# Converting weights in 512-word pieces on three engines, a two-step PReLU, a gram in two row tiles, and a first product from 256 tokens

## The chip, the cores and the metric

One core of a Trainium2 chip runs the whole program. The metric is the device time of one execution in microseconds (us). A profile is one execution taken with the trace; its *span* is the time that the records cover, some 1.7 us less than the time of the same run. Engines: PE is TensorE (matmul), PEld its weight load, DVE is VectorE, ACT is ScalarE, POOL is GpSimd, SP (SPq) issues transfers. A run counts as slow when it is over 1.5% above the fastest of the same kernel; ratios use the fast runs alone.

## The reference

Two stages. First a state-space scan (4 batches, 8 heads, 768 tokens, head size 32, state size 16): in each chunk a "gram" C·Bᵀ is multiplied by a matrix of decay products and applied to x, and a state is carried from chunk to chunk. Its 3072 x 256 result feeds a feed-forward block:

```python
def _moe_ref(x, w_in, w_out, alpha):          # 3072x256, 256x2048, 2048x256, 2048
    h = x @ w_in
    g = np.maximum(h, 0.0) + alpha * np.minimum(h, 0.0)
    return (g @ w_out).astype(np.float32)
```

`w_in` and `w_out` arrive in 64-bit floats, so that the kernel must make 32-bit floats of raw words on the chip. alpha lies between 0 and 0.3.

## The kernel before

A *pair* is two chunks of 128 tokens of the scan. A *group* is two pairs, 512 tokens: 16 hidden tiles (the first product, two matmuls each into one PSUM tile), then 64 matmuls of the second product (27.6 us). An fp32 matmul shows as two records in the trace, so a hidden tile is four, and a group's second product 128. There are six groups. While PE works on one group's hidden tiles, the pairs of the next are mixed in; the stretch of a group with one such pair and eight hidden tiles is called a *half*.

```python
ps_s = ...(name="ps_s", bufs=4, space=PSUM)   # everything of the scan
ps_h = ...(name="ps_h", bufs=2, space=PSUM)   # hidden tiles
ps_o = ...(name="ps_o", bufs=2, space=PSUM)   # output tiles
# ... weights: 32 pieces of 256 words: seven VectorE steps, then one add on GpSimd
# ... gram: four row tiles of 32 rows, for both chunks at once
m = work.tile([P, 2, H, Q], F32, name="m")
gram = [ps_s.tile([P, 2, 2 * Q], F32, name="ss") for r in range(4)]
# ... m = gram * dec on VectorE, four steps
def hidden(g, q):
    for j in range(FQ):
        # ... two matmuls into hp
        nc.scalar.activation(out=gt[:, j], in_=hp, func=ACTF.Relu)
        nc.scalar.activation(out=neg, in_=hp, func=ACTF.Relu, scale=-1.0)
        nc.vector.scalar_tensor_tensor(out=gt[:, j], in0=neg, scalar=nalpha[:, f : f + 1],
                                       in1=gt[:, j], op0=ALU.mult, op1=ALU.add)
# ... main loop
for i in range(GC // 2):          # both pairs of the first group, then all of w_in
    ssm(i); weights(in_pieces, i, GC // 2)
for g in range(NG):               # only then hidden tiles, 512 tokens each
    ...
```

Of the kernel before, what the change touches and what calls it, by code (L numbers as in the profile page):

```python
# [10 lines left out]
U32 = mybir.dt.uint32  # L11
ALU = mybir.AluOpType
ACTF = mybir.ActivationFunctionType

F64_INF, F64_ZERO = (struct.unpack("f", struct.pack("I", w))[0] for w in (0x47F00000, 0x38000000))
# [4 lines left out]
def kernel(  # L20
# [45 lines left out]
    wld = ctx.enter_context(tc.tile_pool(name="wld", bufs=3))  # L66
    wtp = ctx.enter_context(tc.tile_pool(name="wtp", bufs=2))
    lda = ctx.enter_context(tc.tile_pool(name="lda", bufs=2))
    ldx = ctx.enter_context(tc.tile_pool(name="ldx", bufs=4))
# [11 lines left out]
    def load_batch(b):  # L81
        ahn = ld.tile([P, S], F32, name="ahn")
        first = a[b, 0:1, :]
        nc.sync.dma_start(
            out=ahn, in_=bass.AP(tensor=first.tensor, offset=first.offset,
                                 ap=[[S, H], [0, N], [1, S]]))
        loads["b", b] = ahn

# [6 lines left out]
    def load_pair(gp):  # L95
        b, c = divmod(2 * gp, CPB)
        nat = ldx.tile([P, 2, 2, H * N], F32, name="nat")
        abc = lda.tile([P, 2, H * Q], F32, name="abc")
        xt = ldx.tile([P, 2, HD], F32, name="xt")
        for k in range(2):  # L100
            sl = slice((c + k) * Q, (c + k + 1) * Q)
            for i, src in enumerate((B, C)):
                nc.sync.dma_start(out=nat[:, i, k].rearrange("p (h n) -> p h n", h=H),
                                  in_=src[b, :, sl, :].rearrange("h p n -> p h n"))
            first = a[b, 0:1, sl]
            nc.sync.dma_start(
                out=abc[:, k].rearrange("p (h t) -> p h t", h=H),
                in_=bass.AP(tensor=first.tensor, offset=first.offset, ap=[[0, P], [S, H], [1, Q]]),
            )
            nc.sync.dma_start(out=xt[:, k].rearrange("p (h d) -> p h d", h=H),  # L110
                              in_=x[b, :, sl, :].rearrange("h p d -> p h d"))
        loads["p", gp] = nat, abc, xt

    load_rows(0)
    load_batch(0)
# [4 lines left out]
    al_n = const.tile([NF, P], F32, name="al_n")  # L120
    nc.sync.dma_start(out=al_n, in_=moe_alpha.rearrange("(k p) -> k p", p=P))
    in_pieces = [
        (w_in[:, k, f0 : f0 + WQ], moe_w_in[k * P : (k + 1) * P], f0)
        for f0 in range(0, d_ff, WQ)
        for k in range(KC)
    ]
    out_pieces = [(w_out[:, f], moe_w_out[f * P : (f + 1) * P], 0) for f in range(NF)]

    def load_weights(dst, src, c0):



        w = dst.shape[-1]
        if src.dtype == F32:
            nc.sync.dma_start(out=dst, in_=src[:, c0 : c0 + w])
            return
        raw = wld.tile([P, WQ, 2], U32, name="raw")
        nc.sync.dma_start(out=raw[:, :w].rearrange("p w t -> p (w t)"),
                            in_=src[:, c0 : c0 + w].bitcast(U32))
        lo, hi = raw[:, :w, 0], raw[:, :w, 1]  # L140
        t = wtp.tile([P, WQ], U32, name="wt")[:, :w]
        r = wtp.tile([P, WQ], U32, name="wr")[:, :w]
        d = dst.bitcast(U32)
        tf = t.bitcast(F32)


        nc.vector.tensor_single_scalar(out=t, in_=hi, scalar=0x7FFFFFFF, op=ALU.bitwise_and)
        nc.vector.tensor_scalar(out=tf, in0=tf, scalar1=F64_INF, scalar2=F64_ZERO,
                                op0=ALU.min, op1=ALU.max)
        nc.vector.tensor_scalar(out=r, in0=t, scalar1=3, scalar2=0x3FFFFFF8,  # L150
                                op0=ALU.logical_shift_left, op1=ALU.bitwise_and)
        nc.vector.scalar_tensor_tensor(out=r, in0=t, scalar=0x40000000, in1=r,  # L152
                                       op0=ALU.bitwise_and, op1=ALU.bitwise_or)
        nc.vector.scalar_tensor_tensor(out=r, in0=hi, scalar=0x80000000, in1=r,
                                       op0=ALU.bitwise_and, op1=ALU.bitwise_or)
        nc.vector.scalar_tensor_tensor(out=r, in0=lo, scalar=29, in1=r,  # L156
                                       op0=ALU.logical_shift_right, op1=ALU.bitwise_or)
        nc.vector.tensor_scalar(out=t, in0=lo, scalar1=28, scalar2=1,
                                op0=ALU.logical_shift_right, op1=ALU.bitwise_and)
        nc.gpsimd.tensor_tensor(out=d, in0=r, in1=t, op=ALU.add)  # L160
# [15 lines left out]
    par = const.tile([P, 2], F32, name="par")  # L176
    bm2 = bmask.rearrange("p (k e d) -> p e k d", e=2, d=D)
    for e in range(2):
        nc.vector.tensor_reduce(out=par[:, e : e + 1], in_=bm2[:, e, :, 0], op=ALU.add,
                                axis=mybir.AxisListType.X)  # L180
# [3 lines left out]
    nalpha = const.tile([P, NF], F32, name="nalpha")  # L184
    alp = ps_s.tile([P, 512], F32, name="ss")
    nc.tensor.transpose(alp[:, :NF], al_n, ident[:NF, :NF])
    nc.vector.tensor_scalar(out=nalpha, in0=alp[:, :NF], scalar1=-1.0, scalar2=None,
                            op0=ALU.mult)


    pre = {}
# [22 lines left out]
    def batch_prep(b):  # L214

        ahn = loads.pop(("b", b))
        d0 = prep.tile([P, S], F32, name="d0")
        d1 = prep.tile([P, S], F32, name="d1")
        nc.vector.tensor_scalar(out=d0, in0=ahn, scalar1=1e-6, scalar2=1.0,
                                op0=ALU.max, op1=ALU.min)  # L220
        nc.gpsimd.memset(d1, 0.0)
        nc.vector.tensor_copy(out=d1[:, ::Q], in_=d0[:, ::Q])
        nc.vector.memset(d0[:, ::Q], 0.0)
        pf = bat.tile([P, S], F32, name="pf")
        nc.vector.tensor_tensor_scan(out=pf, data0=d0, data1=d1, initial=0.0,
                                     op0=ALU.mult, op1=ALU.add)
        pre[b] = pf

    def pair(gp):

        b, c = divmod(2 * gp, CPB)
        if c == 0:
            batch_prep(b)
        pf = pre[b]
        nat, abc, xt = loads.pop(("p", gp))
# [3 lines left out]
        nc.gpsimd.tensor_scalar(out=abc, in0=abc, scalar1=1.0, scalar2=1e-6,  # L239
                                op0=ALU.min, op1=ALU.max)  # L240
        nc.gpsimd.memset(abc[:, :, ::Q], 0.0)  # L241
        dec = work.tile([P, 2, H, Q], F32, name="dec")
        for k in range(2):
            nc.vector.tensor_tensor_scan(out=dec[:, k].rearrange("p h t -> p (h t)"),  # L244
                                         data0=abc[:, k], data1=ident_h, initial=0.0,
                                         op0=ALU.mult, op1=ALU.add)
# [11 lines left out]
        cz = work.tile([P, 2, 2, Q], F32, name="cz")  # L258
        for e in range(2):
# [3 lines left out]
                                in1=pf[:, c * Q : (c + 2) * Q], op=ALU.mult)  # L263
# [18 lines left out]
        for k in range(nk):  # L282
# [4 lines left out]
            e = (c + k + 1) * Q - 1  # L287
# [6 lines left out]
        m = work.tile([P, 2, H, Q], F32, name="m")  # L294
        gram = [ps_s.tile([P, 2, 2 * Q], F32, name="ss") for r in range(4)]
        for k in range(2):
            for r in range(4):
                rs = slice(32 * r, 32 * r + 32)
                nc.tensor.matmul(gram[r][:, k], bh[rs, k], cz[rs, :, k], start=True, stop=True,  # L299
                                 tile_position=(32 * r, 0), skip_group_check=True)  # L300
        for r in range(4):
            hs = slice(2 * r, 2 * r + 2)
            nc.vector.tensor_tensor(out=m[:, :, hs].rearrange("p k h t -> p k (h t)"), in0=gram[r],  # L303
                                    in1=dec[:, :, hs].rearrange("p k h t -> p k (h t)"),
                                    op=ALU.mult)
# [9 lines left out]
        for k in range(2):  # L315
            for w in range(KC):
                for q in range(4):
                    h = 4 * w + q
                    nc.tensor.matmul(y[32 * q : 32 * q + 32, w, k], xt[:, k, h * D : (h + 1) * D],  # L319
                                     m[:, k, h], start=False, stop=True,  # L320
# [10 lines left out]
    def hidden(g, q):  # L331
        gt = gp.tile([P, FQ, GT], F32, name="gt")
        for j in range(FQ):
            f = q * FQ + j
            hp = ps_h.tile([P, GT], F32, name="hp")
            for k in range(KC):
                nc.tensor.matmul(hp, w_in[:, k, f * P : (f + 1) * P], xts[g][:, k],  # L337
                                 start=(k == 0), stop=(k == KC - 1))
            neg = op.tile([P, GT], F32, name="neg")
            nc.scalar.activation(out=gt[:, j], in_=hp, func=ACTF.Relu)  # L340
            nc.scalar.activation(out=neg, in_=hp, func=ACTF.Relu, scale=-1.0)  # L341
            nc.vector.scalar_tensor_tensor(out=gt[:, j], in0=neg, scalar=nalpha[:, f : f + 1],  # L342
                                           in1=gt[:, j], op0=ALU.mult, op1=ALU.add)
        gts[g, q] = gt
# [15 lines left out]
    def ssm(gp):  # L360
        if gp + 1 < NP:
            load_pair(gp + 1)
        if gp % 3 == 1 and gp // 3 + 1 < batch:
            load_batch(gp // 3 + 1)
# [6 lines left out]
    def weights(lst, i, n):  # L371
        for p in lst[i * len(lst) // n : (i + 1) * len(lst) // n]:
            load_weights(*p)

    for i in range(GC // 2):
        ssm(i)
# [39 lines left out]
```

## Time and profile before

| | before |
|---|---|
| time, median of 3 | 495.63 us (494.58 to 495.81) |
| span of the profiled run | 492.1 us |
| first hidden matmul starts | 54.49 us |
| first group's output ends (last second product of group 1) | 164.66 us |
| from there to the end, "the second part" | 327.44 us |

Busy times by stretch, of the kernel before. The columns are the stretch, its length, then busy us and number of instructions of PE, PEld, DVE, ACT and POOL, then PE's granted clock, the share of the transfer engines, and GB/s:

```profile
0.00:54.49 54.49, 26.48 (x140) 16.96 (x140) 41.01 (x93) 7.40 (x20) 21.53 (x29) 0.84 0.80 180
54.49:164.66 110.17, 83.42 (x313) 49.99 (x312) 103.89 (x222) 21.00 (x40) 39.27 (x38) 0.83 0.54 123
164.66:492.10 327.44, 317.70 (x1451) 209.88 (x1451) 129.78 (x172) 98.34 (x189) 13.16 (x16) 1.00 0.12 28
```

The reader should compare PE and DVE with the length. In the middle stretch DVE is busy 103.89 of 110.17 us and PE 83.42 at a clock of 0.83: DVE bounds. In the last PE is busy 317.70 of 327.44 us: PE bounds.

### The profile page before, as it was taken

What the parts mean: (1) busy time and instruction counts of PE and PEld (TensorE: products, weight loads), DVE (VectorE), ACT (ScalarE), POOL (GpSimd) and SP (SyncE); (2) the same over time, 40 slices, a digit from 0 to 9 for tenths busy, and PEclk for the clock granted to TensorE, in tenths of its full rate; (3) what the DMA queues carried; (4) which work ended last, traced back from release to release, by engine and by line L of the source; (5) the groups of instructions that cost most, each with busy time, mean ns of one, the idle gap of its engine ahead of it and who ended that gap; (6) DMA issues with size and microseconds to landing.
All of it is one profiled execution on the core that took longest, in us unless ns stands there. A gap on an engine that the chain in (4) does not pass through costs nothing.

```text
span 492.1 us, 5000 instructions
## 1 busy us (share of the span) xinstructions
PE 427.6 (87%) x1899; PEld 276.8 (56%) x1899; DVE 274.7 (56%) x485; ACT 126.7 (26%) x249; POOL 74.0 (15%) x81
## 2 busy tenths in 40 slices
PE   0574865983879998999999999999999899999997
PEld 0343433432448644688454886446884448854685
DVE  2699997999899959401877105593024530024300
ACT  2010301420230163400346102643004450046300
POOL 2553543225132210101021000000000000000000
PEclk9985967995699999999999999999999999999999
DMA  6978878544314333200534000000000000000000
GB/s 128 216 170 184 178 185 157 107 118 149 71 38 147 82 92 47 82 23 21 91 60 107 1 22 23 0 1 1 23 21 0 1 0 1 21 23 0 0 23 21
DMA packets 108536, 32.42 MB, mean 66 GB/s; under 512 B 76048, under 2 KB 103904, under 8 KB 108512
## 3 DMA queue, kind: packets, MB, share of 16 engines
q1 hardware_dynamic: 108512, 32.10, 28.4%
q8 instruction: 15, 0.25, 0.2%
q14 instruction: 9, 0.07, 0.1%
HBM read 28.94 MB, written 3.15 MB: 65 GB/s over the span
## 4 chain that ended last, share of the span: by engine, by line
PE 58%; DVE 2%; ACT 0%; issue 0%
PE po L353 28%; PE hp L337 25%; PE ss L319 2%; PE ss L312 1%; DVE m L303 1%; PE ss L276 1%; PE ss L299 1%; PE ss L253 0%; DVE dm L278 0%; DVE state L288 0%; DVE gt L342 0%; ACT gt L340 0%; ACT neg L341 0%; DVE cd L262 0%; DVE o_sb L355 0%
## 5 line engine op out<-in xcount | busy, mean ns | idle before, releaser
L337 PE MATMUL hp<-xT,w_in 128*128 128x512 f32 x384 | 174.8, 605 | 5.2 <-ACT neg L341 5.1
L353 PE MATMUL po<-w_out,gt 128*128 128x256 f32 x768 | 170.2, 381 | 6.8 <-POOL w_out L160 5.8
L353 PEld LDWEIGHTS po<-w_out,gt 128*128 128x128 f32 x768 | 145.8, 191 | 33.9 <-POOL w_out L160 11.2
L337 PEld LDWEIGHTS hp<-xT,w_in 128*128 128x128 f32 x384 | 71.7, 191 | 89.1 <-issue 64.2
L342 DVE SCALAR_TENSOR_TENSOR gt<-neg,nalpha,gt 128x512 f32<-128x512 f32 x96 | 79.4, 833 | 66.9 <-ACT neg L341 66.5
L340 ACT ACTIVATE gt<-hp 128x512 f32<-128x512 f32 x96 | 57.3, 597 | 123.2 <-PE hp L337 123.2
L355 DVE COPY o_sb<-po 128x256 f32<-128x256 f32 x24 | 10.1, 421 | 122.5 <-PE po L353 122.4
L341 ACT ACTIVATE neg<-hp 128x512 f32<-128x512 f32 x96 | 56.8, 592 | 13.5 <-DVE gt L342 13.5
L244 DVE TENSOR_TENSOR_SCAN dec<-abc,ident_h 128x1024 f32<-128x1024 f32 x24 | 55.4, 2337 | 1.6 <-POOL abc L241 1.0
L299 PE MATMUL ss<-cz,bh 32*128 32x256 f32 x192 | 32.8, 464 | 19.3 <-DVE cd L262 16.0
L257 ACT COPY bh<-ss 128x256 f32<-128x256 f32 x12 | 4.5, 375 | 141.9 <-PE ss L253 141.9
L299 PEld LDWEIGHTS ss<-cz,bh 32*128 32x128 f32 x192 | 20.1, 211 | 34.2 <-DVE cd L262 19.0
L239 POOL TENSOR_SCALAR abc<-abc 128x2048 f32<-128x2048 f32 x12 | 25.2, 2098 | 85.4 <-DMA abc<-in_a_dram 71.6
L303 DVE TENSOR_TENSOR m<-ss,dec 128x512 f32<-128x512 f32 x48 | 30.4, 681 | 2.2 <-PE ss L299 2.2
L269 POOL TENSOR_TENSOR bn<-nat,prt 128x256 f32<-128x256 f32 x12 | 10.6, 883 | 85.7 <-PE ss L276 52.5
L319 PE MATMUL ss<-m,xt 128*32 128x128 f32 x384 | 21.1, 310 | 1.9 <-DVE m L303 1.9
L160 POOL TENSOR_TENSOR w_out<-wr,wt 128x256 uint32<-128x256 uint32 x16 | 15.8, 985 | 43.4 <-DVE wr L156 43.4
L325 ACT COPY xT<-ss 128x512 f32<-128x512 f32 x12 | 7.1, 589 | 55.8 <-PE ss L319 55.8
L160 POOL TENSOR_TENSOR w_in<-wr,wt 128x256 uint32<-128x256 uint32 x16 | 16.4, 1023 | 29.6 <-DVE wr L156 29.5
L319 PEld LDWEIGHTS ss<-m,xt 128*32 128x32 f32 x384 | 12.1, 118 | 12.8 <-issue 6.1
L312 PE MATMUL ss<-cd,state 128*128 128x128 f32 x64 | 11.1, 326 | 8.4 <-DVE m L303 8.4
L152 DVE SCALAR_TENSOR_TENSOR wr<-wt,wr 128x256 uint32<-128x256 uint32 x32 | 16.7, 521 | 0.0
(47 smaller groups left out, 183.4 us busy)
## 6 DMA issues: line engine op xcount, KB each, us to landing
abc<-in_a_dram SPq DMA_DIRECT2D x24, 512.0 KB, 5.0
raw<-in_moe_w_in_dram SPq DMA_DIRECT2D x16, 256.0 KB, 3.9
raw<-in_moe_w_out_dram SPq DMA_DIRECT2D x16, 256.0 KB, 2.6
xt<-in_x_dram SPq DMA_DIRECT2D x24, 128.0 KB, 3.3
out_dram<-o_sb SPq DMA_DIRECT2D x12, 256.0 KB, 2.1
ahn<-in_a_dram SPq DMA_DIRECT2D x4, 384.0 KB
nat<-in_B_dram SPq DMA_DIRECT2D x24, 64.0 KB, 3.1
nat<-in_C_dram SPq DMA_DIRECT2D x24, 64.0 KB, 2.8
```

Of the source, the lines that this page charges most:

```text
L152: nc.vector.scalar_tensor_tensor(out=r, in0=t, scalar=0x40000000, in1=r, op0=ALU.bitwise_and, op1=ALU.bitwise_or)
L160: nc.gpsimd.tensor_tensor(out=d, in0=r, in1=t, op=ALU.add)
L239: nc.gpsimd.tensor_scalar(out=abc, in0=abc, scalar1=1.0, scalar2=1e-6, op0=ALU.min, op1=ALU.max)
L244: nc.vector.tensor_tensor_scan(out=dec[:, k].rearrange("p h t -> p (h t)"), data0=abc[:, k], data1=ident_h, initial=0.0, op0=ALU.mult, op1 ...
L299: nc.tensor.matmul(gram[r][:, k], bh[rs, k], cz[rs, :, k], start=True, stop=True, tile_position=(32 * r, 0), skip_group_check=True)
L303: nc.vector.tensor_tensor(out=m[:, :, hs].rearrange("p k h t -> p k (h t)"), in0=gram[r], in1=dec[:, :, hs].rearrange("p k h t -> p k (h t)"),
L319: nc.tensor.matmul(y[32 * q : 32 * q + 32, w, k], xt[:, k, h * D : (h + 1) * D], m[:, k, h], start=False, stop=True, tile_position=(0, 32 ...
L337: nc.tensor.matmul(hp, w_in[:, k, f * P : (f + 1) * P], xts[g][:, k], start=(k == 0), stop=(k == KC - 1))
L340: nc.scalar.activation(out=gt[:, j], in_=hp, func=ACTF.Relu)
L341: nc.scalar.activation(out=neg, in_=hp, func=ACTF.Relu, scale=-1.0)
L342: nc.vector.scalar_tensor_tensor(out=gt[:, j], in0=neg, scalar=nalpha[:, f : f + 1], in1=gt[:, j], op0=ALU.mult, op1=ALU.add)
L353: nc.tensor.matmul(po[:, :d_model], gts[g, f // FQ][:, f % FQ, ts], w_out[:, f], start=(f == 0), stop=(f == NF - 1))
```

## The change

Its intent: relieve VectorE in the first part (bigger pieces, three steps in place of seven on it), start PE earlier (256 tokens, two weight pieces), and relieve ScalarE and VectorE in the PReLU and the gram. Cut to its core:

```diff
-        nc.vector.tensor_single_scalar(out=t, in_=hi, scalar=0x7FFFFFFF, op=ALU.bitwise_and)
 ...    (six more VectorE steps for 256 words)
-        nc.gpsimd.tensor_tensor(out=d, in0=r, in1=t, op=ALU.add)
+        nc.scalar.activation(out=tf, in_=hi.bitcast(F32), func=ACTF.Abs, scale=0.125)
+        nc.vector.tensor_scalar(out=tf, in0=tf, scalar1=F64_INF, scalar2=F64_ZERO, ...)
+        nc.scalar.activation(out=g, in_=half, func=ACTF.Copy, scale=2.0**-11, bias=2.0**25)
+        if sg is None:      # w_in
+            nc.gpsimd.tensor_scalar(out=r, in0=hi.bitcast(F32), scalar1=0.0, scalar2=2.0**31,
+                                    op0=ALU.is_lt, op1=ALU.mult)          # the sign
+        else:               # w_out
+            for i in range(2):
+                nc.vector.tensor_scalar(out=r[:, i], in0=hi[:, i], scalar1=SIGN, scalar2=sg[i], ...)
+        nc.vector.scalar_tensor_tensor(out=r, in0=t, scalar=3, in1=r, ...)  # shift and combine
+        nc.vector.tensor_tensor(out=d, in0=r, in1=g.bitcast(U32), op=ALU.add)

-            nc.scalar.activation(out=gt[:, j], in_=hp, func=ACTF.Relu)
-            nc.scalar.activation(out=neg, in_=hp, func=ACTF.Relu, scale=-1.0)
-            nc.vector.scalar_tensor_tensor(out=gt[:, j], in0=neg, scalar=nalpha[:, f : f + 1],
-                                           in1=gt[:, j], op0=ALU.mult, op1=ALU.add)
+            nc.scalar.mul(gt, hp, s_alpha[:, f : f + 1])
+            nc.vector.scalar_tensor_tensor(out=gt, in0=hp, scalar=s_mul[:, f : f + 1], in1=gt,
+                                           op0=ALU.mult, op1=ALU.max)

-        gram = [ps_s.tile([P, 2, 2 * Q], F32, name="ss") for r in range(4)]
 ...    (16 matmuls of 32 rows; product into m)
+        for k in range(2):
+            gram = [ps_s.tile([P, 4, Q], F32, name="ss") for r in range(2)]
 ...        (two matmuls of 64 rows)
+                nc.vector.tensor_tensor(out=dec[:, k, hs], in0=gram[r], in1=dec[:, k, hs], ...)

+    ssm(0)
+    for q in range(NQ):     # two w_in pieces, then four hidden tiles of 256 tokens; pair 1 after q = 0
+        ...
+    for q in range(NQ):     # two w_out pieces, then the other 256 tokens; pairs 2 and 3 between
+        ...
```

The whole diff holds smaller parts too: the decays are loaded and scanned for each pair and no longer for each batch, GpSimd clamps the decays of one chunk at a time, the first loads of B and C go to ScalarE's queue, and two pools change their number of buffers.

## The prediction

> **What bounds the kernel now**
>
> I read the strip of 40 slices first, to see whether one engine bounds the whole span, and then busy times by stretch.
>
> ```profile
> PE   0574865983879998999999999999999899999997
> ...
> DVE  2699997999899959401877105593024530024300
> ...
> PEclk9985967995699999999999999999999999999999
> DMA  6978878544314333200534000000000000000000
> ...
> 50.00:75.00 25.00, 19.48 (x77) 10.54 (x75) 24.38 (x56) 5.07 (x10) 13.23 (x12) 0.78 0.83 186
> ...
> 100.00:125.00 25.00, 13.82 (x38) 7.36 (x38) 24.39 (x57) 2.15 (x4) 9.71 (x10) 0.74 0.41 122
> ...
> 271.60:299.20 27.60, 27.60 (x130) 24.25 (x130) 2.20 (x5) 1.08 (x2) 0.00 (x0) 1.00 0.03 10
> 299.20:338.30 39.10, 38.34 (x188) 19.26 (x186) 27.66 (x34) 19.36 (x38) 1.66 (x2) 1.00 0.02 8
> ```
>
> There are two kernels in one. Up to about 150 us DVE is at 9 nearly throughout (24.4 of 25 us) while PE has holes and runs at a clock of 0.59 to 0.9: DVE bounds. From then on PE is full at clock 1.00 and bounds. The chain that ended last says the same: from 188 us on it is almost only PE.
>
> ```profile
> 271.59 27.63 PE po L353 x128
> 299.21 0.44 PE ss L253 x4
> 299.65 0.43 PE ss L276 x2
> 300.08 0.86 PE hp L337 x2
> 300.94 1.31 PE ss L299 x14
> 302.25 0.69 DVE m L303
> ...
> 302.98 1.16 PE ss L312 x8
> ...
> 306.54 12.21 PE hp L337 x28
> ```
>
> A group of 512 tokens is 27.63 us of second product, then twice a half of one pair's scan work mixed with eight hidden tiles. A hidden tile is four records, 27.47/16 = 1.717 us. From 299.21 to 306.54 is 7.3 us with one hidden tile in it, then seven tiles, 12.2: a half is 19.5, a group 66.6 us.
>
> What DVE does in the first part, and what it holds in the second:
>
> ```profile
> L342 DVE SCALAR_TENSOR_TENSOR gt<-neg,nalpha,gt 128x512 f32<-128x512 f32 x96 | 79.4, 833 | 66.9 <-ACT neg L341 66.5
> ...
> L154 DVE SCALAR_TENSOR_TENSOR wr<-raw,wr 128x256 uint32<-128x256 uint32 x32 | 13.6, 426 | 0.0
> ...
> L150 DVE TENSOR_SCALAR wr<-wt 128x256 uint32<-128x256 uint32 x32 | 11.6, 361 | 0.0
> ...
> 304.81 4.47 DVE L244 TENSOR_TENSOR_SCAN dec<-abc,ident_h 128x1024 f32<-128x1024 f32 x2
> 309.20 1.39 DVE L342 SCALAR_TENSOR_TENSOR gt<-neg,nalpha,gt 128x512 f32<-128x512 f32 x2
> 311.32 0.75 DVE L342 SCALAR_TENSOR_TENSOR gt<-neg,nalpha,gt 128x512 f32<-128x512 f32 x1 [0.74 <-ACT neg L341]
> ```
>
> The reader should see that two decay scans (4.47 us) hold up two PReLU steps until 309.20, and that PE doesn't notice (12.21 us without a gap): DVE doesn't free the PSUM tile today, ScalarE does.
>
> **What the Trainium skill says**
>
> - "VectorE: DVE Perf Modes", the perf-mode tier table: in fp32 a one-input op between SBUF tiles runs at 2×, a two-input one or one with a PSUM operand at 1×. The trace agrees: starts of undisturbed 256-word one-input ops lie 0.20 us apart, of two-input ones 0.34.
> - "SBUF — State Buffer", Who interferes with whom: DVE ops in a 2-port mode or with two SBUF inputs lock out GpSimd reads and the reverse. It agrees: one POOL add in the conversion took 2.97 us at 30.70 beside a scan, against 0.73 alone; one DVE op 1.98 against 0.28 beside a POOL clamp of 2.02.
> - "ScalarE: Activation LUTs", What ACT_TABLE_LOAD costs: a per-partition pointer operand adds about 93 ns. The 128x256 cz step with a pointer is 486 ns, the bh copy without 375: agrees. So the new ScalarE step is about 0.60 + 0.09 = 0.69 us.
> - "TensorE: Matmul & The Clock Gate", Part 3, Packing small matmuls: row tiles overlap. The 16 gram records of a pair ran in 1.15 us when nothing held them; one after the other they would take 16 x 0.213 = 3.4. With two row tiles instead of four I estimate 3.4/2 = 1.7 us.
>
> **The change part by part**
>
> *Conversion.* Before: 32 pieces, each four one-input and three two-input DVE ops, start to start 4 x 0.20 + 3 x 0.34 = 1.82 us, 58 us (84 us as the groups sum, with GpSimd's lock). After: 16 pieces of 512 words; on DVE a clamp (about 0.34), a shift-and-combine (0.60, as a 128x512 two-input op: 2.48/4 at 302.23) and an integer add now on DVE, which no row shows; I take 0.60. 1.54 us; for w_out two sign steps of 0.20 more. 8 x 1.54 + 8 x 1.94 = 28 us: 30 us less DVE, in the part that DVE bounds. ScalarE gets 32 steps of 0.6, 19 us, into an engine at 2 to 5 us of 25; GpSimd gets eight sign steps in place of 32 adds.
>
> *Order.* The first product now starts with 256 tokens and two pieces instead of after two pairs and all of w_in (54.5 us in the trace). By the built order the queue brings 0.06 MB of rows and alpha, two pairs of 1.7 MB, two pieces of 0.52 MB: 4.5 MB. With DMA full (share 1.00 in 12 to 25 us) the trace moved 220 GB/s: 20.5 us, plus 2 for the start, plus about 4 for conversion: 27 us.
> From there I added up DVE's built order, line by line with the start-to-start times, to the last decay product of pair 3: 8 us for the rest of pair 1, 3 + 8 + 6 for the other w_in pieces, the first half of the PReLU steps (about 0.36 each at 256 tokens) and pair 2, 14 and 20 for w_out, the second half and pair 3: 59 us, so 86 us. DMA must bring 8.4 MB of weights and some 7.7 MB of pairs by the last piece: 16.1/0.22 = 73 us when full, 91 us at the 0.8 share it had from 25 to 75. I take the later, 91. Then PE still has some 48 second products (0.432 each, 21) and the end of pair 3 (5): the first group's output ends at about **117 us**, against 164.6 before. The gain here is **48 us**. PE's own work to there is 27.5 + 27.6 + 4 x 5.4 = 77 us; before it was busy 110 us for it, 33 of them from the low clock, and idle 55.
>
> *PReLU.* Two ScalarE steps and a DVE step become one and one. ScalarE's 114 us (96 x 2 steps) become 80 x 0.69 plus 32 half ones, about 70. But the DVE step now reads the PSUM tile itself: with two such tiles, PE may fill the third only when DVE is through with the first. Cycle: 1.717 fill + 0.69 + about 0.72 on DVE + some 0.15 of handovers = 3.28, under 2 x 1.717 = 3.43. So PE stays the bound, with only 0.15 us to spare. The decay product is now written in place, so the next scan into that buffer waits for PE's last use of it, and in DVE's order both scans stand just before the second PReLU step of the half. From the end of the pair's matmuls: scans until 4.5, PReLU until 5.3; PE fills two tiles until 3.43 and then waits: **1.9 us** per half. Six halves have such scans (pairs 6 to 11): 11.5 us.
>
> *Gram.* 1.7 for 1.15 to 1.5 us on PE, and cz four steps for two on ScalarE (off the path). DVE's order also puts two short scans and a PReLU step ahead of the first decay product; I get 7.75 us from the pair's transposes to its last matmul, against 7.4. Eight halves x 0.35 = 3 us.
>
> Sum after the first group: a group is 2 x (7.75 + 1.9 + 12.0) + 27.6 = 71 us three times, 67 for the fourth, 55.1 for the last, 3.6 of tail, and 1 for odds: 339 to **340 us**, against 327.5 before (492.1 - 164.6). 117 + 340 = 457 us of span. Timed runs lie 3.5 us over the span (495.63 to 492.1): **460 us**, 7% faster.
>
> **The rivals**
>
> 1. *DVE becomes the bound of the second part too.* For: it now frees every hidden tile, has 37 us of work in a 43 us stretch, and long scans stand in its order. Against: the cycle of 3.28 fits. If the PReLU step takes 0.9 us instead of 0.72, the cycle is 3.46 and costs little; if each scan stalls PE by its full 4.4 us, add 6 x 2.5 = 15: 475.
> 2. *The first part doesn't shrink, as DMA or handovers bound it.* For: a piece passes ScalarE, GpSimd and DVE, each in strict order with only two buffers, and DMA was at 0.83 already. If the first group ends at 140, 483: within 2% nearly.
> 3. *The first part shrinks to its DVE sum.* DMA kept full, PE warm: 105 us, 448.
> 4. *Stalls don't show*, because the scans start before PE is through: then 446.
>
> **Range and chances**
>
> Rivals 1 and 2 together would be needed for no gain. The first part carries the larger doubt (105 to 135), the second part 10 us either way: 443 to 478. Faster by over 2% means under 485.7.
>
> **What would show each step right or wrong**
>
> Right: the first hidden matmul at about 27 us; DVE conversion near 28 us; first group's output ending at 117; then PE waiting for the DVE PReLU step about 2 us once per half, right after the scans, in groups 1 to 3 and not in the last two; groups of 71 us. Wrong: a group still at 66.6 (the stall is hidden), PE waits at every hidden tile (the cycle is over 3.43), PE clock low or DMA share under 0.7 in the first 90 us (waits, not work, bound the first part), or an integer add well over 0.6.

## The result, and the profile after

The changed kernel took **472.66 us** (median of 4 runs, 471.05 to 473.84), all correct, against 495.5 us for the kernel before in the same rounds: ratio 0.954, 95% interval 0.951 to 0.957. Ratios here are the mean time of one kernel's fast runs over that of the other's of the same rounds, so they aren't quite the ratio of the medians. The predicted class was right, and 472.66 lies inside the range of 443 to 478, but 12.7 us above the 460 predicted.

The strip of 40 slices of the changed kernel, 11.8 us each (busy tenths; PEclk the granted clock):

```profile
PE   1788679999989799998989998989999999999996
DVE  2998779899584830065840065840043530034200
PEclk9868889999999999999999999999999999999999
DMA  9995668935643430034330030000000000000000
```

PE is now nearly full from the seventh slice on, where before it was from about the thirteenth. But DVE isn't at 9 in slices five and six (7 and 7), nor is DMA (6 and 6), and the clock is still low there: something waits. And later PE has slices at 8 where the kernel before had 9s. Busy times by stretch:

```profile
0.00:30.26 30.26, 15.11 (x64) 7.78 (x65) 19.96 (x34) 9.62 (x24) 16.10 (x23) 0.87 0.95 195
30.26:72.00 41.74, 31.62 (x121) 17.96 (x120) 32.44 (x57) 18.82 (x37) 19.01 (x15) 0.81 0.66 176
72.00:128.89 56.89, 55.45 (x290) 41.92 (x291) 49.92 (x86) 17.76 (x37) 14.18 (x17) 1.00 0.68 156
128.89:471.60 342.71, 324.08 (x1396) 203.79 (x1393) 130.92 (x188) 73.93 (x128) 13.60 (x24) 1.00 0.14 30
```

The first group's output ends at 128.89 us, 35.8 us earlier than before (117 was predicted: 47.7). The second part takes 342.71 us, 15.3 more than before (340 was predicted: 12.6 more). So of 35.8 us won, 15.3 are given back. Two questions follow: what costs the missing 12 us in the first part, and is it the PReLU that gives back the 15 in the second?

**First part.** Between 30.26 and 72 us DVE is busy only 32.44 of 41.74 us and PE 31.62. Timeline of all engines in that stretch (start, length, engine, line, what it does; in brackets the idle time just before, and what ended it):

```profile
46.01 4.92 POOL L167 TENSOR_SCALAR wr<-raw 128x512 uint32<-128x512 f32 x2 [6.47 <-DVE w_in L176]
49.06 1.11 DVE L173 SCALAR_TENSOR_TENSOR wr<-wt,wr 128x512 uint32<-128x512 uint32 x1 [1.85 <-POOL wr L167]
50.97 0.69 DVE L173 SCALAR_TENSOR_TENSOR wr<-wt,wr 128x512 uint32<-128x512 uint32 x1 [0.80 <-POOL wr L167]
52.11 2.72 PE L352 MATMUL hp<-xT,w_in 128*128 128x256 f32 x8 [4.13 <-DVE gt L356]
```

This is a ping-pong. GpSimd waits 6.47 us for DVE's add to give back one of two sign buffers, makes two signs in 4.92 us, DVE waits for each, and the PReLU steps (L356) stand behind them in DVE's order, so that PE waits 4.13 us. The sign step by itself, its eight records as minimum, median and maximum in ns:

```profile
L167 POOL TENSOR_SCALAR wr<-raw x8: 1937/2032/3011, 22.4 to 59.7; 128x512 uint32<-128x512 f32 x8
```

Even the quickest took 1.94 us.

**Second part.** One half of the third group (PE L352 are hidden matmuls, DVE L258 the decay scans, DVE L356 the PReLU):

```profile
209.66 3.70 PE L352 MATMUL hp<-xT,w_in 128*128 128x512 f32 x8
209.85 4.47 DVE L258 TENSOR_TENSOR_SCAN dec<-abc,ident_h 128x1024 f32<-128x1024 f32 x2 [0.27 <-PE ss L332]
...
214.43 1.40 DVE L356 SCALAR_TENSOR_TENSOR gt<-hp,s_mul,gt 128x512 f32<-128x512 f32 x2
...
215.22 7.25 PE L352 MATMUL hp<-xT,w_in 128*128 128x512 f32 x16 [1.87 <-DVE gt L356]
```

PE fills two hidden tiles while the scans run, then waits 1.87 us until DVE has got to the PReLU of the first. Five other halves show the same wait, 1.66 us each; the halves of the last two groups have no scans beside them, and no such wait. The six add to 10.2 us.

### The profile page after: what moved, and what is told of

Same layout as the page of the kernel before. It is cut to its first block, busy times and chain, and to the rows that moved or that the text cites. A ratio compares the mean times of both kernels' runs of the same rounds, so it can differ in the third digit from the quotient of the medians.

```text
span 471.6 us, 4815 instructions
## 1 busy us (share of the span) xinstructions
PE 426.3 (90%) x1867; PEld 271.4 (58%) x1867; DVE 233.2 (49%) x363; ACT 120.1 (25%) x225; POOL 62.9 (13%) x78
## 3 DMA queue, kind: packets, MB, share of 16 engines
HBM read 28.94 MB, written 3.15 MB: 68 GB/s over the span
## 4 chain that ended last, share of the span: by engine, by line
PE 66%; DVE 15%; issue 9%; ACT 3%; DMA 3%; POOL 2%; SPq 0%; DVEq 0%; POOLq 0%; ACTq 0%
PE po L366 31%; PE hp L352 28%; DVE dec L258 5%; DVE gt L356 3%; PE ss L332 2%; DVE dec L317 2%; POOL wr L167 2%; PE ss L325 1%; DVE pf L249 1%; PE ss L312 1%; ACT gt L355 1%; ACT cz L274 1%; DMA ap<-in_a_dram 1%; PE ss L290 1%; DMA abc<-in_a_dram 1%
## 5 line engine op out<-in xcount | busy, mean ns | idle before, releaser
L352 PE MATMUL hp<-xT,w_in 128*128 128x512 f32 (+1 forms) x448 | 184.9, 560 | 20.1 <-DVE gt L356 18.1
L352 PEld LDWEIGHTS hp<-xT,w_in 128*128 128x128 f32 x448 | 81.9, 197 | 112.8 <-DVE gt L356 52.4
L356 DVE SCALAR_TENSOR_TENSOR gt<-hp,s_mul,gt 128x512 f32<-128x512 f32 (+1 forms) x112 | 74.2, 670 | 79.8 <-ACT gt L355 79.4
L355 ACT ACTIVATE gt<-hp,s_alpha 128x512 f32<-128x512 f32 (+1 forms) x112 | 70.0, 627 | 146.6 <-PE hp L352 146.4
L368 DVE COPY o_sb<-po 128x256 f32<-128x256 f32 x24 | 10.2, 423 | 124.6 <-PE po L366 124.6
L258 DVE TENSOR_TENSOR_SCAN dec<-abc,ident_h 128x1024 f32<-128x1024 f32 x24 | 55.4, 2331 | 3.3 <-PE ss L332 3.3
L255 POOL TENSOR_SCALAR abc<-abc 128x1024 f32<-128x1024 f32 x24 | 30.3, 1261 | 112.2 <-DMA abc<-in_a_dram 81.4
L312 PE MATMUL ss<-cz,bh 64*128 64x512 f32 x96 | 33.5, 695 | 6.1 <-DVE cd L276 4.1
L317 DVE TENSOR_TENSOR dec<-ss,dec 128x512 f32<-128x512 f32 x48 | 30.5, 680 | 0.6 <-PE ss L312 0.6
L167 POOL TENSOR_SCALAR wr<-raw 128x512 uint32<-128x512 f32 x8 | 17.4, 2192 | 16.6 <-DVE w_in L176 12.9
L274 ACT ACTIVATE cz<-ss,par 128x256 f32<-128x256 f32 x48 | 19.4, 485 | 0.0
L332 PE MATMUL ss<-dec,xt 128*32 128x128 f32 x384 | 17.0, 292 | 2.2 <-DVE dec L317 2.2
L173 DVE SCALAR_TENSOR_TENSOR wr<-wt,wr 128x512 uint32<-128x512 uint32 x16 | 12.5, 787 | 5.0 <-POOL wr L167 5.0
L159 ACT ACTIVATE wt<-raw 128x512 f32<-128x512 f32 x16 | 10.7, 675 | 15.9 <-DMA raw<-in_moe_w_in_dram 10.9
(46 smaller groups left out, 129.8 us busy)
```

The source lines that it names most:

```text
L167: nc.gpsimd.tensor_scalar(out=r, in0=hi.bitcast(F32), scalar1=0.0, scalar2=2.0**31, op0=ALU.is_lt, op1=ALU.mult)
L255: nc.gpsimd.tensor_scalar(out=abc[:, k], in0=abc[:, k], scalar1=1.0, scalar2=1e-6, op0=ALU.min, op1=ALU.max)
L258: nc.vector.tensor_tensor_scan(out=dec[:, k].rearrange("p h t -> p (h t)"), data0=abc[:, k], data1=ident_h, initial=0.0, op0=ALU.mult, op1 ...
L274: nc.scalar.mul(cz[:, e].rearrange("p k t -> p (k t)"), ct, par[:, e : e + 1])
L312: nc.tensor.matmul(gram[r].rearrange("p h t -> p (h t)"), bh[rs, k], cz[rs, :, k], start=True, stop=True, tile_position=(64 * r, 0), skip_ ...
L317: nc.vector.tensor_tensor(out=dec[:, k, hs], in0=gram[r], in1=dec[:, k, hs], op=ALU.mult)
```

## The experiments

Twelve kernels ran, three rounds each, all with correct results. "First" is the end of the first group's output and "second" the rest of the span, both from the one profiled run.

| kernel | median us (range) | ratio to before (95%) | first | second |
|---|---|---|---|---|
| changed kernel | 472.66 (471.05 to 473.84) | 0.954 (0.951 to 0.957) | 128.9 | 342.7 |
| sign_dve | 468.04 (462.89 to 469.26) | 0.945 (0.938 to 0.952) | 121.9 | 344.0 |
| prelu_old | 458.57 (457.64 to 458.90) | 0.928 (0.925 to 0.931) | 128.6 | 328.2 |
| gram4 | 479.59 (478.36 to 480.75) | 0.970 (0.967 to 0.974) | 133.2 | 345.6 |
| dec3 | 475.26 (470.63 to 477.44) | 0.961 (0.954 to 0.967) | 131.1 | 343.7 |
| share | 456.51 (455.04 to 459.15) | 0.924 (0.918 to 0.929) | 125.4 | 327.8 |
| sign_prelu | 453.12 (447.97 to 455.13) | 0.909 (0.902 to 0.916) | 118.1 | 328.1 |
| conv_old | 506.61 (504.60 to 508.49) | 1.024 (1.019 to 1.030) | 160.7 | 342.2 |
| order_old | 477.08 (474.31 to 477.95) | 0.963 (0.957 to 0.968) | 132.2 | 344.0 |
| sign_share | 451.21 (449.87 to 455.97) | 0.914 (0.906 to 0.921) | 122.6 | 327.8 |
| m_apart | 470.00 (468.08 to 472.66) | 0.950 (0.946 to 0.955) | 126.9 | 339.5 |
| sign_prelu_gram4 | 457.68 (451.80 to 459.40) | 0.921 (0.914 to 0.928) | 119.9 | 330.2 |
| sign_share_order | 457.81 (455.30 to 458.37) | 0.924 (0.920 to 0.928) | 129.8 | 326.2 |

Two of the four runs of sign_prelu and one of sign_prelu_gram4 count as slow and are in the medians but not in the ratios; the other kernels had fast runs only. The first part scatters by some 4 us from one profiled run to another (126.9 to 131.1 in the changed kernel, dec3 and m_apart, which hardly differ there); the second part repeats within about 2 us (342.2 to 344.0 in the changed kernel, sign_dve, dec3, conv_old and order_old). The runs were made on several chips, each against the kernel before on the same chip, so the ratios are the safer comparison.

### sign_dve: the sign step on VectorE

```diff
-            nc.gpsimd.tensor_scalar(out=r, in0=hi.bitcast(F32), scalar1=0.0, scalar2=2.0**31,
-                                    op0=ALU.is_lt, op1=ALU.mult)
+            nc.vector.tensor_single_scalar(out=r, in_=hi, scalar=SIGN, op=ALU.bitwise_and)
```

> The changed kernel with one step moved: the sign step of the w_in conversion (eight times 128x512) goes from GpSimd to VectorE, as a bitwise AND. In the changed kernel this step took 2.19 us on GpSimd beside VectorE's work and stood in the chain that ended last between 35 and 62 us, and the first group's output ended at 128.9 us where 117 was predicted. Theory A (the handover to a GpSimd that VectorE locks out is what costs those 12 us): the first group's output ends at 117 to 122 us, the kernel is 7 to 12 us faster, near 462 us. Theory B (VectorE's sum of work or the transfers bound the first part anyway): eight steps of about 0.35 us more on VectorE, so within 2 us of the changed kernel's 472.7, first output at 127 to 132 us. The second part is unchanged in both, 343 us.

The first output ended at 121.85 us, in the range of theory A; the time fell by 4.6 us, less than its 7 to 12, and the intervals of the two ratios just touch. Beside the old PReLU the same edit is clear of noise (sign_prelu 0.902 to 0.916, prelu_old 0.925 to 0.931). Busy times of the stretch from the first hidden matmul on:

```profile
28.39:60.00 31.61, 23.31 (x115) 15.01 (x115) 30.14 (x57) 18.15 (x38) 6.70 (x8) 0.89 0.95 251
```

DVE is busy 30.14 of 31.61 us (95%, where it was 32.44 of 41.74, 78%, in the changed kernel) and the transfers run at 0.95 in place of 0.66. The step itself:

```profile
L167 DVE TENSOR_SCALAR wr<-raw 128x512 uint32<-128x512 uint32 x8 | 3.3, 414 | 0.0
```

414 ns on VectorE for 2192 on GpSimd. So the handover to GpSimd was a cost, and VectorE's sum of work is the next bound: up to the last decay product of the fourth pair at 98.87 us it was busy 68.93 of 70.48 us. One part of my theory falls: it isn't VectorE's lock that makes the step slow. Among 56 records of it, in seven kernels that keep it on GpSimd, none took less than 1.937 us, and the one at 37.60 us of the changed kernel took 1.947 us although VectorE was busy during only 0.60 us of it. Whether the operation, its reading of every second word or the change of type costs that was not tested.

### prelu_old: the old PReLU

```diff
-            nc.scalar.mul(gt, hp, s_alpha[:, f : f + 1])
-            nc.vector.scalar_tensor_tensor(out=gt, in0=hp, scalar=s_mul[:, f : f + 1], in1=gt, ... max)
+            nc.scalar.activation(out=gt, in_=hp, func=ACTF.Relu)
+            nc.scalar.activation(out=neg, in_=hp, func=ACTF.Relu, scale=-1.0)
+            nc.vector.scalar_tensor_tensor(out=gt, in0=neg, scalar=nalpha[:, f : f + 1], in1=gt, ... add)
```

(It is right for these data, whose alpha are all below 1.)

> The changed kernel with the old PReLU: two Relu steps on ScalarE, which free the hidden PSUM tile, and one VectorE step that reads SBUF only. Theory A (the second part's 15 us over the kernel before are the hidden PSUM tiles that VectorE now frees late: six stalls of 1.66 us after the scans and 0.05 us for each of 80 tiles): both vanish, seven hidden tiles take 12.2 us again, the second part is 328 to 332 us. Theory B (the second part lost its time to the two-row-tile gram and the product in place): the second part stays at 340 us or more. The first part gets more ScalarE work but no more VectorE work and should move by less than 4 us. In all 458 to 462 us under A, 470 to 474 under B.

458.57 us, second part 328.18: theory A in every number. The first part didn't move (128.6), so no gain of the new PReLU shows there either.

### share: one set of four PSUM banks for hidden and output tiles

```diff
-    ps_h = ctx.enter_context(tc.tile_pool(name="ps_h", bufs=2, space=PSUM))
-    ps_o = ctx.enter_context(tc.tile_pool(name="ps_o", bufs=2, space=PSUM))
+    ps_h = ctx.enter_context(tc.tile_pool(name="ps_h", bufs=4, space=PSUM))
-                po = ps_o.tile([P, 512], F32, name="po")
+                po = ps_h.tile([P, GT], F32, name="hp")
```

> The changed kernel, PReLU untouched, but the two hidden PSUM tiles and the two output PSUM tiles come from one set of four banks, so that up to four hidden tiles can be open and no bank is added. Theory A (VectorE frees the hidden tile, and two tiles are too few for its cycle and for two scans in a row): the waits of 1.66 us after the scans and the 0.05 us per tile vanish although the PReLU is the new one; second part 328 to 333 us against 342.7, in all 458 to 463 us, as with the old PReLU (458.6). Theory B (it is VectorE's or ScalarE's own work in the new PReLU that costs, not the number of tiles): second part stays over 338 us, in all 468 or more.

This tells "two tiles are too few" from "the new steps are too slow", since it keeps the steps. 456.51 us, second part 327.79: theory A, both slightly better than its ranges. The half that was shown of the changed kernel, now:

```profile
201.72 12.28 PE L351 MATMUL hp<-xT,w_in 128*128 128x512 f32 x28
201.91 4.47 DVE L257 TENSOR_TENSOR_SCAN dec<-abc,ident_h 128x1024 f32<-128x1024 f32 x2 [0.27 <-PE ss L331]
...
206.49 2.16 DVE L355 SCALAR_TENSOR_TENSOR gt<-hp,s_mul,gt 128x512 f32<-128x512 f32 x3
```

DVE does the same as before (scans of 4.47 us right after the pair, then the PReLU steps, now three in a row), but PE runs 28 hidden matmuls without a gap. So the place of the scans and the length of the steps are harmless by themselves; with two tiles they aren't. The groups of 512-token hidden matmuls, first of the changed kernel, then of this one (busy us, mean ns, idle before):

```profile
L352 PE MATMUL hp<-xT,w_in 128*128 128x512 f32 x320 | 145.6, 605 | 10.2 <-DVE gt L356 10.2
```

```profile
L351 PE MATMUL hp<-xT,w_in 128*128 128x512 f32 x320 | 141.1, 595 | 0.0
```

The idle 10.2 us are gone, and so are 4.5 us of busy time. I read these as PE being held up a little at each tile, without an idle record.

### m_apart and dec3: what holds the scans

```diff
 m_apart
+        m = mp.tile([P, 2, H, Q], F32, name="m")          # one buffer
-                nc.vector.tensor_tensor(out=dec[:, k, hs], in0=gram[r], in1=dec[:, k, hs], ...)
+                nc.vector.tensor_tensor(out=m[:, k, hs], in0=gram[r], in1=dec[:, k, hs], ...)
 dec3
-        dec = work.tile([P, 2, H, Q], F32, name="dec")    # two buffers
+        dec = decp.tile([P, 2, H, Q], F32, name="dec")    # three buffers
```

> The changed kernel with the decay product written to a tile of its own instead of in place, so that the next scans wait only for VectorE's own products and no longer for PE's use of them. Theory A (the in-place product is what holds the scans back, by 0.27 to 0.60 us in the trace): each stall of 1.66 us shrinks by that much or more, to 1.0 to 1.4, second part 1.5 to 5 us shorter. Theory B (the scans come when VectorE's order lets them, as with the third decay buffer, which changed nothing): stalls stay at 1.66, within 2 us of the changed kernel.

> The changed kernel with a third buffer for the decay tile. Since the product is written in place, a scan can start only when the matmuls of two pairs before are through with the tile; with a third buffer that wait falls away. Theory A (the scan's wait for the buffer sets how late the PReLU steps come): the stalls of 1.66 us after the scans shrink to under 0.5 us, 5 to 10 us faster. Theory B (VectorE runs its instructions in program order, and both scans stand just ahead of the second PReLU step whatever the buffers; they would wait for the same place in the order): stalls stay near 1.7 us, within 2 us of the changed kernel.

With the product apart the scans of the same half start without a wait, and the stall is 1.48 in place of 1.87 us; the five others are 1.15 or 1.16 in place of 1.66:

```profile
206.23 4.45 DVE L259 TENSOR_TENSOR_SCAN dec<-abc,ident_h 128x1024 f32<-128x1024 f32 x2
...
211.57 2.84 PE L354 MATMUL hp<-xT,w_in 128*128 128x512 f32 x6 [1.48 <-DVE gt L358]
```

The second part is 3.2 us shorter, of which the six stalls make 2.9 (10.2 to 7.2 us): theory A, but it is a third of the stall. The timed runs (470.00 us) can't show so little: the intervals overlap. The third buffer brought no gain (475.26 us, its interval overlapping too; five stalls of 1.66 to 1.86 us): theory B. Its scans were ordered one pair further ahead, and there they wait again for PE's last use of the pair just finished:

```profile
213.31 4.47 DVE L259 TENSOR_TENSOR_SCAN dec<-abc,ident_h 128x1024 f32<-128x1024 f32 x2 [0.27 <-PE ss L333]
```

More buffers let the program's order run further ahead; they didn't move the scans away from the place where they hurt.

### gram4 and sign_prelu_gram4: the gram in four row tiles

```diff
-        for k in range(2):
-            gram = [ps_s.tile([P, 4, Q], F32, name="ss") for r in range(2)]
+        gram = [ps_s.tile([P, 2, 2 * Q], F32, name="ss") for r in range(4)]
 ...    (16 matmuls of 32 rows in place of four of 64 x 512; two masked copies of C in place of four;
         four products for both chunks, still in place)
```

> The changed kernel with the four row tiles for the gram restored (16 matmuls of 32 rows for each pair, two masked copies of C on ScalarE instead of four), the product still in place. Theory A (the gram in two row tiles costs PE 0.3 to 0.8 us more in each of six halves and in the first part's pairs, and no more): 1 to 5 us faster, 468 to 471. Theory B (the gram is the cause of most of the second part's 15 us): 10 us faster or more. The stalls of 1.66 us after the scans stay under A.

> Sign step on VectorE, old PReLU, and the gram in four row tiles: against the same kernel with two row tiles (453.1). With the new PReLU the four tiles were 7 us slower (479.6 for 472.7), about 4 in the first part and 3 in the second, which I hadn't expected. Theory A (four row tiles hold all four PSUM tiles until VectorE is through, and fewer of them are free for the next pair, whatever the PReLU): again 4 to 8 us slower, 457 to 461. Theory B (it only collided with the late freeing of hidden tiles): within 2 us of 453. Theory C (the two-row-tile gram costs PE more, as predicted: 0.3 us more in each half): 1 to 4 us faster.

I had expected the two-row-tile gram to cost time. Putting the four tiles back made the kernel 7 us *slower*, which fits neither theory, and again slower (ratio 0.921 for 0.909, though the intervals overlap a little) beside the old PReLU. In the traces the second part is 2.9 and 2.0 us longer; the rest of the 7 us lies in the first part (133.2 for 128.9), where the scatter is as large. The same half, first in sign_prelu with two row tiles, then in sign_prelu_gram4 with four:

```profile
189.12 1.99 PE L313 MATMUL ss<-cz,bh 64*128 64x512 f32 x8
191.03 0.71 PE L326 MATMUL ss<-cd,dm 128*128 128x128 f32 x4
```

```profile
190.54 1.98 PE L315 MATMUL ss<-cz,bh 32*128 32x256 f32 x16
193.28 0.71 PE L327 MATMUL ss<-cd,dm 128*128 128x128 f32 x4 [0.75 <-DVE dec L320]
```

The gram takes 2.0 us in both here (1.38 to 1.85 with four tiles in the other halves of that kernel), but after four tiles PE waits for DVE's first decay products before it goes on; after two it doesn't in this half. Over the second part PE's waits, as the timelines list them, add to 2.76 us with two tiles and 6.98 with four: 4.2 us more, against 2.8 us that the eight grams save (13.1 for 15.9). My reading is that four tiles at once take all four PSUM tiles of the scan, so that the next matmul must wait for the first product, while two and two are freed in turn. The waits are shown; that this is their cause is argued from the code. Beside the new PReLU the listed waits hardly differ (15.85 us in gram4, 14.84 in the changed kernel), so what makes gram4 slower there stays open.

### conv_old and order_old: the two halves of the first part's gain

```diff
 conv_old                               (on 512-KB pieces and the new order)
+        for i in range(2):
 ...        (seven VectorE steps of 256 words, GpSimd's add, as in the kernel before)
 order_old
-    ssm(0)
-    for q in range(NQ): ...            (256 tokens)
+    for i in range(GC // 2):           # both pairs, all of w_in
+        ssm(i)
+        for p in in_pieces[4 * i : 4 * i + 4]: load_weights(...)
+    ...                                # then tiles of 512 tokens
```

> The changed kernel with the old conversion: each 512-word piece as two times seven VectorE steps and one GpSimd add, on the changed kernel's transfers and order. It measures what the new conversion is worth by itself. The prediction's sum: VectorE gets 30 us more (58 for 28) in a part that VectorE bounds; with GpSimd's lock it was 84 busy us before for 38 after. Theory A (the first part follows VectorE's sum): 25 to 40 us slower, 498 to 513. Theory B (the order hides it, PE having enough to do meanwhile): under 15 us slower. The second part should stay at 343 us.

> The changed kernel with the old order of the main loop: both first pairs and all of w_in, then tiles of 512 tokens. It measures what starting from 256 tokens is worth by itself. Theory A (PE idles until w_in is there and its clock stays low, as in the kernel before): the first hidden matmul at 38 to 45 us in place of 30, the first group's output 8 to 20 us later, 480 to 492. Theory B (the first part is bound by VectorE's sum, and the order only shifts PE's work): within 5 us of 472.7.

The old conversion costs 34 us (theory A), nearly all in the first part (160.7 for 128.9); with it the other changes together are 2.4% slower than the kernel before (interval 1.9 to 3.0%, so unclear at the 2% limit). The old order costs 4.4 us (theory B), barely clear of noise: the first hidden matmul came at 46.7 us, later than theory A said, yet the first group's output only 3.3 us later. So the conversion made the gain, and the early start little of it: 31.8 and 3.3 of the first part's 35.8 us.

### sign_prelu, sign_share and sign_share_order: the repairs together

> Sign step on VectorE and the old PReLU, all else as changed. If the two repairs lie in different parts and add up: 468.0 and 458.6 against 472.7 give 454 us, with the first group's output ending near 122 us and a second part near 328 us. If the old PReLU's extra ScalarE work delays the conversion steps on ScalarE once GpSimd is out of the way: 457 to 459.

> The two repairs that keep the new PReLU: sign step on VectorE, and one set of four PSUM banks for hidden and output tiles. The gains of the two alone against the changed kernel's 472.7 were 4.6 us (468.0) and 16.2 us (456.5). If they lie in different parts and add up: 450 to 454, first group's output at 118 to 122 us, second part 328. That would equal or beat the old PReLU with the same sign step (453.1). If VectorE, which has four hidden tiles to serve and the sign steps, becomes the bound: 455 or more.

> Sign step on VectorE, four shared PSUM banks, new PReLU, but the old order of the main loop. With the changed kernel the order was worth about 4 us (477.1 for 472.7). Theory A (the first part is set by VectorE's sum of work, so that the order of PE's work in it moves little): 2 to 6 us slower than the same kernel with the new order. Theory B (with VectorE relieved of GpSimd's lock, an early first product pays more): 8 us slower or more.

Both sums hold: 453.12 us (454 expected; its two fast runs took 447.97 and 451.51) and 451.21 us (450 to 454). They can't be told apart by these runs, which were on two chips, but both beat the changed kernel by about 20 us and take about 9% less than the kernel before. Busy times of sign_share:

```profile
28.56:60.00 31.44, 25.59 (x131) 17.69 (x131) 28.64 (x57) 20.18 (x42) 5.76 (x7) 0.95 0.87 241
60.00:122.60 62.60, 54.24 (x282) 41.41 (x283) 54.67 (x93) 16.02 (x34) 14.89 (x20) 0.95 0.65 147
122.60:450.40 327.80, 319.59 (x1395) 207.81 (x1393) 130.91 (x188) 73.93 (x128) 13.01 (x22) 1.00 0.14 31
```

PE is busy 319.59 of 327.80 us in the second part; what is left is in the first. With these repairs the old order costs 6.6 us in place of 4.4, just above theory A's 2 to 6.

## Why the prediction was right or wrong

The class and the range held because the largest term, VectorE's conversion work in a part that VectorE bounds, was right in kind and nearly in size. Counted from the start of each instruction to the start of the next or to its own end, the traces give 67 us before and 34 after, 33 us less where 30 was predicted. (The groups of the profile sum to 84.0 and 37.9, so "near 28" did not show: the combining step, for one, took 787 ns on average and 680 at the end of the conversion. The integer add came as assumed, 0.60 us from start to start there.) The 12.7 us come from these terms (us). The measured column adds up: 98.2 + 9.7 + 21.0 is the first group, and 327.4 of the kernel before + 10.2 + 4.7 + 0.4 the second part; 4.7 is what the stalls leave of the difference to share's groups. The predicted column doesn't quite add up: 327.4 + 11.5 + 3 is 341.9, since the prediction's sum by groups leaves out about 2 us that the kernel before has too:

| term, as the prediction put it | predicted | measured |
|---|---|---|
| first hidden matmul | 27 | 30.3 |
| last weight piece through | 91 | 98.2 |
| from there to the last decay product of the fourth pair | 0 (its 86 was held to be earlier) | 9.7 |
| PE's rest of the first group | 26 | 21.0 |
| first group's output ends | 117 | 128.9 |
| stalls after the scans | 11.5 | 10.2 |
| hidden cycle over 3.43 us | 0 | about 4.7 |
| gram and its products | 3 | about 0.4 |
| second part | 340 | 342.7 |
| timed median over span | 3.5 | 1.1 |

**"Ends at 117" failed, and it is the step that made most of the miss.** The sum counted GpSimd's eight sign steps as nothing ("GpSimd gets eight sign steps in place of 32 adds"). They took 2.19 us each, in a ping-pong with VectorE. Moved to VectorE, the last piece is through at 89.2 us, near the predicted 91, and the first output is at 121.9; with the old PReLU as well, at 118.1. Rival 2, handovers through strict order with two buffers, had named this, but with a first group that ends at 140, outside the 105 to 135 that the prediction allowed for. What remains is an error of order: I took the later of 86 (VectorE) and 91 (transfers), as if the fourth pair's work could be done before the last piece. In VectorE's order its scans and products stand behind that piece, 9.7 us, in the changed kernel and in sign_dve alike. VectorE has no idle moment in this stretch of the changed kernel (columns as above):

```profile
98.20:107.90 9.70, 8.56 (x58) 6.10 (x57) 9.70 (x15) 0.95 (x2) 0.00 (x0) 1.00 0.31 93
```

That is read from the traces; no run moved them. An opposite error, 26 for 21 us of rest on PE, hid half of it; that the gram and the step from span to time were also put too high (2.6 and 2.4 us) is luck of the same kind. (The 3.5 us from span to time set the median of the timed runs against the span of another run; the profiled run itself took 493.78 us.) The sign that the prediction set for this, a clock low or a "DMA share under 0.7 in the first 90 us", showed in part: the share was 0.66 between 30 and 72 us, at a clock of 0.81, but 0.82 over the whole 90 us.

**The stall was right** in place (after the scans), in number (six halves, none in the last two groups) and nearly in size (1.66 and once 1.87 for 1.9 us). The three groups with stalls took 72.0 us on average for the 71 predicted, the fourth 67.1 for 67. share shows its cause to be the two PSUM tiles, and m_apart that the product in place makes up 0.4 to 0.5 us of each.

**"Cycle 3.28, under 3.43" was mis-sized.** The steps came as assumed, 687 ns on ScalarE and 747 on VectorE (0.69 and 0.72), but with PE's 1.717 us they make 3.15, and the 0.15 of handovers was too little: the hidden tiles of the last two groups, which have no stall, take 0.70 and 0.80 us longer than in share, about 0.05 us for each of their 16 tiles. With two tiles in turn that makes a cycle of some 3.53 us, so 0.38 of handovers (an estimate from these figures).

**The gram's +3 us was wrong as a sum**: prelu_old, which differs from the kernel before in the second part mainly by the gram and the product in place, takes 328.2 us there for 327.4, and share 327.8. On PE the 3 us are there: eight grams of 1.99 us make 15.9 us for 12.8 before. What the prediction left out is that PE's waits for the products fall as well, from 5.88 us in the kernel before to 2.75 in prelu_old.

Of the rivals, 1 (VectorE bounds the second part) and 4 (no stalls; its 446 is a span, the time would be 449) did not come; 3 (VectorE's plain sum, ending at 105) was too hopeful, since even with VectorE 98% busy the end was 121.9.

## What to carry to other kernels

When a step that frees a PSUM tile moves from one engine to another, put the new engine's longest uninterrupted work against the number of open tiles: with two tiles PE had 3.7 us of work beside two scans of 4.5 us and then waited, with four from the same banks it ran through. An engine that looks idle isn't free: here a step of 0.41 us on VectorE took 2.2 on GpSimd, and with two buffers in strict order three engines waited for it. And undo each part of a change alone: here one part (the conversion) earned more than the whole, and another (the PReLU) gave 14 us back.

## What the Trainium skill lacked or had wrong

- "GPSIMD Engine Reference", 4.1 Engine selection, puts one-input elementwise work there at roughly line rate. The packed fp32 clamp fits (1.04 us for 1024 elements), but the sign step (compare and multiply, fp32 at every second word in, uint32 out) took 1.94 us at its quickest for 512 elements, 3.7 times as long per element; the same sign on VectorE took 0.41.
- "VectorE: DVE Perf Modes", the table of specifications, calls integer operands exact below 2^24 only. The kernel's 32-bit integer add on VectorE gave right results; the trace shows it as a custom instruction over 1024 16-bit elements, 0.68 us for 512 words. That need not contradict the page, since 16-bit elements lie below the limit; I found no page that tells of this instruction or its time.
- No page that I read says what a step that frees a PSUM tile costs when the tiles number just enough: 0.05 us for each of 16 tiles a group with two tiles and steps that add to 3.15 us, where PE fills two tiles in 3.43.
